# Both ends of a TensorE-bound block: the last 256 tokens in two groups of 128, the first transposes spread between products

## The chip, the cores and the metric

The kernel runs on one core of one Trainium2 chip. The metric is device microseconds (us) of one execution, as the median of several runs. The profile is one execution; its span, from the first to the last instruction, is 1.7 to 2.0 us shorter than the time of the same run. Engines: TensorE (PE; PEld is its weight load), VectorE (DVE), ScalarE (ACT), GpSimd (POOL) and SyncE (SP), whose queue issues most DMAs. All runs here are of the fast state, at a granted clock of 0.995 to 1.0. A ratio is the mean time of one kernel's fast runs over that of the kernel before in the same rounds, so it is not quite the ratio of the medians that are quoted.

## The reference, cut to what matters

```python
def reference(A_x, A_wqkv, A_wo, B_x, B_w1, B_w3, B_w2):
    x  = A_x                                  # (1, 2048, 1024) bf16
    xn = _layernorm(x)
    s  = _A_ref(xn, A_wqkv, A_wo)             # dilated window attention, then @ wo
    g  = _silu(_B_ref(xn, B_w1, B_w3, B_w2))  # gated MLP, width 3584
    return x + s * g
```

Two things of it are concerned: the front (layernorm of the first 512 tokens, their transposes, the first products with `wqkv`) and the very end, where the product with `wo` is multiplied by `g`, the input `x` is added, and the result is written.

## The kernel before

The products are done with a seven-product scheme on halves of the matrices, so that each output piece is a PSUM sum plus an earlier one. Front, end and the statistics of the third and fourth chunk of 512 tokens (condensed; cuts are marked `# ...`):

```python
def tpose(st, a):                     # both halves of a token tile in one PSUM tile
    if st not in tpb:
        tpb[st] = bank2(f"tp{st}")
    for k in range(KH):
        anchor["t"] = nc.tensor.matmul(tpb[st][:, a, k * P:(k + 1) * P], lhsT=..., rhs=ident[:], ...)
# ...
p12(0, 0, one, (0,))
p12(0, 0, one, (1,))
tpose(2, 0); tpose(2, 1); tpose(3, 0); tpose(3, 1)      # third and fourth token tile
untp(2, 0, sc_copy); untp(2, 1, dve_copy)               # copies out of PSUM
untp(3, 0, sc_copy); untp(3, 1, dve_copy)
p12(1, 0, one)
# ...
def tr(c):                            # statistics and transposes of a later chunk
    for sts in ([0, 1], [2, 3]):
        ln_dve(c, sts)
    ln_tr(c, ...)
# ...
for gp in G2:                         # wo: two groups of 256 tokens in each half b
    product(both(pa), gp, a11, b11, True)
    product(both(pe), gp, s1, t1, True)
    flush()                           # last product of the previous group
    # ... act_copy pa -> pb, act_copy pe -> sp5
    product(pbs, gp, s2, t2, False)
    # ... act_copy pb -> su2
    product(both(pe), gp, s4, b22, False);  finished(b, 0, 1, gp, pe, su2[:])
    product(pbs, gp, s3, t3, False);        finished(b, 1, 1, gp, pb, sp5[:])
    product(both(pa), gp, a12, b21, False); finished(b, 0, 0, gp, pa)
    # deferred: product(pbs, gp, a22, t4, False); finished(b, 1, 0, gp, pb)
```

`finished` turns the PSUM sum into bf16 (`d`), multiplies it by `g`, adds `x` (`xw`) and issues the output write. For the last group all of that lies on DVE, with ScalarE for the copies, and the writes go out on the SP queue.

## Time and profile before

| before | us |
|---|---|
| time, median of three runs | 723.84 (723.78 to 724.5) |
| last matmul ends / DVE ends | 715.89 / 718.69 |
| last output write issued / landed | 718.85 / 720.62 |
| span ends | 721.8 |

Read the table from below: after its last matmul the kernel needs another 5.9 us. 3.0 of them pass until the last write is issued, 1.8 until it has landed, and 1.2 until the program ends. The lines that carry the bound and the front are shown with the prediction. One more view of the kernel before matters later: the DMA view of the stretch from 718 to 722 us. Its rows have 40 slices of 0.1 us: the busy share of the DMA engines in tenths, and the rate in GB/s. Below stand the output writes issued in the stretch, with their count, size and time from issue to landing.

```profile
DMA  0000006999999999627995000000000000000000
GB/s 0 0 0 0 0 0 246 399 369 389 389 369 389 389 369 399 205 82 276 379 420 164 10 0 0 0 0 0 0 0 0 0 0 0 0 0 0 0 0 0
...
out_dram<-h_sb SPq DMA_DIRECT2D x2, 128.0 KB, 1.8
```

The data of the last writes come as a block that ends as sharply as it began, at 720.3 us.

### The profile page before, as it was taken

To read this page: it belongs to the slowest core of one execution; us is meant where nothing else is said; L and a number is where in the kernel's file an instruction comes from. 1 tells how busy PE (TensorE), PEld (TensorE's weight loads), DVE (VectorE), ACT (ScalarE), POOL (GpSimd) and SP (SyncE) were. 2 spreads that over 40 slices of the span, in tenths; PEclk is the share of its full clock that TensorE was granted. 3 is DMA by queue.
4 is the path that set the end of the run, shared out by engine and by line. 5 is a ranking of instruction groups with operands and counts; after the bars stand their busy time and mean duration, and the time that the engine had idled before them with its cause. 6 is when DMAs were issued, how large, how long until landed. Compare 5 with 4: busy or idle time off the path is not lost.

```text
span 721.8 us, 8746 instructions
## 1 busy us (share of the span) xinstructions
PE 710.0 (98%) x3313; PEld 346.2 (48%) x3367; DVE 624.9 (87%) x690; ACT 312.9 (43%) x326; POOL 95.7 (13%) x162
## 2 busy tenths in 40 slices
PE   8999999999999999999999999999999999999996
PEld 6655565654444444444444444444444444444442
DVE  7996879779879878978999999969859989999974
ACT  5745334356545456555555312034364573020233
POOL 0011100012300000233111000000435004000011
PEclk9999999999999999999999999999999999999999
DMA  9946257777754523558756547469799444563615
GB/s 337 275 125 182 82 185 228 258 249 238 246 172 153 191 71 117 173 191 268 246 174 216 190 132 250 144 205 385 168 276 336 139 138 150 168 202 129 199 36 108
DMA packets 119193, 139.51 MB, mean 193 GB/s; under 512 B 17648, under 2 KB 94448, under 8 KB 118512
## 3 DMA queue, kind: packets, MB, share of 16 engines
q1 hardware_dynamic: 104608, 97.01, 42.6%
q0 software_dynamic: 14544, 41.95, 18.0%
q8 instruction: 26, 0.43, 0.2%
q14 instruction: 15, 0.12, 0.1%
HBM read 96.21 MB, written 38.80 MB: 187 GB/s over the span
## 4 chain that ended last, share of the span: by engine, by line
PE 95%; ACT 2%; DVE 2%; issue 1%; DMA 0%; DVEq 0%; ACTq 0%
PE bm L151 20%; PE am L151 13%; PE em L151 13%; PE db L151 10%; PE bq L151 9%; PE de L151 7%; PE da L151 7%; PE eq L151 5%; PE aq L151 3%; PE wb L151 2%; PE af L151 2%; PE we L151 2%; PE wa L151 2%; DVE h_sb L236 1%; PE af L1049 1%
## 5 line engine op out<-in xcount | busy, mean ns | idle before, releaser
L151 PEld LDWEIGHTS <-wring 128*128 128x128 f16 (+1 forms) x1792 | 183.4, 102 | 204.3 <-issue 2.2
L151 PEld LDWEIGHTS <-h_sb 128*128 128x128 f16 (+1 forms) x1056 | 109.5, 104 | 118.4 <-issue 0.6
L151 PE MATMUL bm<-xs,wring 128*128 128x512 f16 x504 | 117.4, 379 | 0.2
L151 PE MATMUL am<-xT,wring 128*128 128x512 bf16 x322 | 79.0, 379 | 0.8
L151 PE MATMUL db<-wring,h_sb 128*128 128x512 f16 x336 | 73.2, 379 | 0.0
L481 DVE TENSOR_TENSOR BC<-Ep,vT 128x2048 bf16<-128x2048 bf16 x56 | 66.6, 1217 | 0.1
L426 DVE TENSOR_TENSOR pt<-qt,kT 128x4096 bf16<-128x4096 bf16 x24 | 54.9, 2290 | 0.6
L664 DVE TENSOR_TENSOR um<-em,um 128x1024 f32<-128x1024 f32 x28 | 34.2, 1222 | 21.0 <-PE em L151 13.3
L666 ACT ACTIVATE g<-um 128x1024 bf16<-128x1024 f32 x28 | 29.6, 1057 | 48.6 <-DVE um L664 48.6
L151 PE MATMUL da<-wring,h_sb 128*128 128x512 bf16 x219 | 48.7, 379 | 0.3
L467 POOL DMA_DIRECT2D Ep<-pb x64 | 38.0, 601 | 53.4 <-DVE pb L463 48.1
L151 PE MATMUL bm<-h_sb,wring 128*128 128x512 f16 x168 | 39.7, 379 | 0.0
L151 PE MATMUL em<-xs,wring 128*128 128x512 f16 x168 | 39.7, 379 | 0.0
L151 PE MATMUL em<-xT,wring 128*128 128x512 bf16 x161 | 39.2, 379 | 0.3
L491 DVE TENSOR_TENSOR oT<-oT,BC 128x2048 bf16<-128x2048 bf16 x32 | 39.0, 1219 | 0.3
L161 ACT COPY bm<-am 128x1024 f32<-128x1024 f32 x28 | 27.9, 998 | 25.9 <-PE am L151 25.9
L161 ACT COPY pm<-em 128x1024 f32<-128x1024 f32 x28 | 28.4, 1013 | 20.1 <-PE em L151 20.1
L161 ACT COPY um<-bm 128x1024 f32<-128x1024 f32 x28 | 28.4, 1014 | 18.9 <-PE bm L151 18.9
L685 ACT CAST g<-bm 128x1024 bf16<-128x1024 f32 x28 | 28.3, 1011 | 17.4 <-PE bm L151 17.4
L679 DVE TENSOR_TENSOR h_sb<-bm,pm 128x1024 bf16<-128x1024 f32 x21 | 25.6, 1218 | 5.1 <-PE bm L151 5.0
L489 DVE TENSOR_TENSOR BC<-BC 128x2048 bf16<-128x2048 bf16 x24 | 29.3, 1221 | 0.4
L428 DVE TENSOR_TENSOR pt<-pt 128x2048 bf16<-128x2048 bf16 x24 | 29.3, 1221 | 0.4
(197 smaller groups left out, 993.5 us busy)
## 6 DMA issues: line engine op xcount, KB each, us to landing
wring<-in_B_w_dram SPq DMA_DIRECT2D x61, 512.0 KB, 4.2
wring<-t_dram SPq DMA_DIRECT2D x16, 512.0 KB, 3.8
t_dram<-wring POOLq DMA_DIRECT2D x14, 512.0 KB, 3.8
wring<-t_dram SPq DMA_DIRECT2D x16, 384.0 KB, 4.9
wring<-in_B_w_dram SPq DMA_DIRECT2D x12, 384.0 KB, 4.5
wring<-in_A_x_dram SPq DMA_DIRECT2D x16, 256.0 KB, 4.2
Ep<-pb POOLq DMA_DIRECT2D x64, 64.0 KB, 4.9
wring<-in_A_wo_dram SPq DMA_DIRECT2D x8, 512.0 KB, 5.6
```

What stands on the lines that cost most here:

```text
L151: anchor["pe"] = nc.tensor.matmul(ps, lhsT=lhs[k], rhs=rhs[k], start=(first and k == 0), stop=(k == n - 1), skip_group_check=not first,)
L161: nc.scalar.copy(out=out_, in_=in_)
L426: nc.vector.tensor_mul(p_t[:], q[:], kT[:, :, o:o + CH])
L428: nc.vector.tensor_add(p_t[:, 0:4, :], p_t[:, 0:4, :], p_t[:, 4:8, :])
L467: nc.gpsimd.dma_start(out=pr[c][r:P:NR, :, sq * P:(sq + 1) * P], in_=pb[sq * 32:(sq + 1) * 32, :, :])
L481: nc.vector.tensor_mul(dst, E[:, w, :].unsqueeze(1).to_broadcast([P, n, CH]), vT[:, js, o:o + CH])
L489: nc.vector.tensor_add(B, B, C)
L491: nc.vector.tensor_add(A, A, B if w0 else C)
L664: v = nc.vector.tensor_add(su2[:], pe[:], su2[:])
L666: nc.scalar.activation(out=hl["g"][:, :, CH:], in_=su2[:], func=ACTF.Silu)
L679: anchor["v"] = nc.vector.tensor_add(h[:, :, CH:], pb[:], sp5[:])
L685: nc.scalar.copy(out=hl["g"][:, :, 0:CH], in_=pb[:])
```

## The change

Its intent: the last 256 tokens become two groups of 128, so that DVE has less work left behind the last matmul; the first transposes get PSUM tiles of their own for each half, and the fourth tile's transposes move between products; an early sum of the `q` weights comes sooner; and the statistics of later chunks are ordered behind the sums. In the small groups the third product comes before the second, and the last output piece goes through a ScalarE copy in both halves, where the kernel before multiplied one half straight out of PSUM. The core of the diff, condensed and with cuts:

```diff
-        for gp in G2:
+        for gp, ii in ((0, I), (1, I)) if b == 0 else ((0, I), (1, (0,)), (1, (1,))):
...
+            for k in ("e12", "e22", "e11") if n == 2 else ("e11", "e22", "e12"):
+                steps[k]()
...
-    tpb[0], tpb[1], tpb[2] = [bank2(f"tp{k}") for k in range(3)]
+    lone = [bank2(f"tp{k}") for k in range(3)]
+    tpb[0, 0], tpb[1, 0], tpb[0, 1], tpb[1, 1] = lone[0][:, 0], lone[1][:, 0], lone[2][:, 0], lone[2][:, 1]
...
+    s_q = qkv_sums(wq0, wq1, sq, parts=True)
+    s_q[0]()
...
     tpose(2, 0)
     tpose(2, 1)
+    untp(2, 0, sc_copy)
+    untp(2, 1, dve_copy)
+    p12(1, 0, one[:2])
     tpose(3, 0)
     tpose(3, 1)
...
-    p12(1, 0, one)
+    p12(1, 0, one[2:])
...
     def tr(c):
         for sts in ([0, 1], [2, 3]):
-            ln_dve(c, sts)
+            with behind("ln"):
+                ln_dve(c, sts)
```

More of the change, by code (lines that the diff above doesn't have):

```diff
@@ L890, in wo, with product @@
                         nc.sync.dma_start(out=xw[u, dh], in_=out_rows(x_flat, 1, u, dh, 1))
-        def product(ps, gp, lhs, rhs, first):
-            for i in I:
+        def product(ps, gp, ii, lhs, rhs, first):
+            for n, i in enumerate(ii):
                 g = gp * 2 + i
-                mm(ps[i], [lhs[:, j, g * P:(g + 1) * P] for j in range(4)], [rhs[:, j, :] for j in range(4)], first)
-        both = lambda t: [t[:, i] for i in I]
-        for gp in G2:
-            run_hooks()
-            last = b == 1 and gp == 1
-            pa = bank2(f"wa{b}_{gp}")
-            product(both(pa), gp, a11, b11, True)
-            pe = bank2(f"we{b}_{gp}")
-            product(both(pe), gp, s1, t1, True)
-            flush()
-            pb = [bank2(f"wb{b}_{gp}{i}")[:, i] for i in I] if last else bank2(f"wb{b}_{gp}")
-            for i in I:
-                if last:
-                    act_copy(pb[i], pa[:, i])
-            if not last:
-                act_copy(pb[:], pa[:])
-            pbs = pb if last else both(pb)
-            sp5, su2 = k4(f"wsp{b}_{gp}"), k4(f"wsu{b}_{gp}")
-            act_copy(sp5[:], pe[:])
-            bg((7, 0)[gp] * (1 - b))
-            product(pbs, gp, s2, t2, False)
-            for i in I:
-                if last:
-                    act_copy(su2[:, i], pb[i])
-            if not last:
-                act_copy(su2[:], pb[:])
-            product(both(pe), gp, s4, b22, False)
-            finished(b, 0, 1, gp, pe, su2[:])
-            product(pbs, gp, s3, t3, False)
-            finished(b, 1, 1, gp, pb, sp5[:])
-            product(both(pa), gp, a12, b21, False)
-            finished(b, 0, 0, gp, pa)
-            def tail(gp=gp, pb=pb, pbs=pbs):
-                product(pbs, gp, a22, t4, False)
-                finished(b, 1, 0, gp, pb)
@@ new lines, in product, with half, tail @@
+                mm(ps[:, n], [lhs[:, j, g * P:(g + 1) * P] for j in range(4)], [rhs[:, j, :] for j in range(4)], first)
+        for gp, ii in ((0, I), (1, I)) if b == 0 else ((0, I), (1, (0,)), (1, (1,))):
+            n = len(ii)
+            name = f"{b}_{gp}{ii[0]}"
+            def half(t):
+                return t[:, 0:n]
+            run_hooks()
+            pa = half(bank2(f"wa{name}"))
+            product(pa, gp, ii, a11, b11, True)
+            pe = half(bank2(f"we{name}"))
+            product(pe, gp, ii, s1, t1, True)
+            flush()
+            pb = half(bank2(f"wb{name}"))
+            act_copy(pb, pa)
+            sp5, su2 = half(k4(f"wsp{name}")), half(k4(f"wsu{name}"))
+            act_copy(sp5, pe)
+            bg((7, 0)[gp] * (1 - b))
+            product(pb, gp, ii, s2, t2, False)
+            act_copy(su2, pb)
+            steps = {
+                "e12": lambda: (product(pe, gp, ii, s4, b22, False), finished(b, 0, 1, gp, ii, pe, su2)),
+                "e22": lambda: (product(pb, gp, ii, s3, t3, False), finished(b, 1, 1, gp, ii, pb, sp5)),
+                "e11": lambda: (product(pa, gp, ii, a12, b21, False), finished(b, 0, 0, gp, ii, pa)),
+            }
+            for k in ("e12", "e22", "e11") if n == 2 else ("e11", "e22", "e12"):
+                steps[k]()
+            def tail(gp=gp, ii=ii, pb=pb):
+                product(pb, gp, ii, a22, t4, False)
+                finished(b, 1, 0, gp, ii, pb)
@@ L939, in out_rows @@
         return ap[g0:g0 + 2 * P, dh * CH:(dh + 1) * CH].rearrange("(i p) n -> p i n", p=P)
-    def to_bf16(d, ps, add):
-        if add is None:
-            nc.scalar.copy(out=d, in_=ps[:])
-        elif isinstance(ps, list):
-            for i in I:
-                nc.vector.tensor_add(d[:, i], ps[i], add[:, i])
-        else:
-            nc.vector.tensor_add(d, ps[:], add)
     xw = {}
@@ L958, in residual, with finished @@
                 nc.sync.dma_start(out=out_flat[r0:r0 + n, dh * CH:(dh + 1) * CH], in_=x_flat[r0:r0 + n, dh * CH:(dh + 1) * CH])
-    def finished(b, u, dh, gp, ps, add=None):
-        g = g_tile(b, u, dh, gp)
+    def finished(b, u, dh, gp, ii, ps, add=None):
+        cut = slice(ii[0], ii[-1] + 1)
+        g = g_tile(b, u, dh, gp)[:, cut]
         n = {(0, 0): 0, (1, 1): 2, (0, 1): 4, (1, 0): 0}[u, dh] + gp
-        d = h_sb[:, 16 + 2 * n:18 + 2 * n, CH:]
-        rows_ = out_rows(out_flat, b, u, dh, gp)
+        d = h_sb[:, 16 + 2 * n:18 + 2 * n, CH:][:, cut]
+        rows_ = out_rows(out_flat, b, u, dh, gp)[:, cut]
         with hp():
+            if add is None:
+                nc.scalar.copy(out=d, in_=ps)
+            else:
+                nc.vector.tensor_add(d, ps, add)
+            anchor["v"] = nc.vector.tensor_mul(g, d, g)
             if b == 0 or gp == 0:
-                to_bf16(d, ps, add)
-                anchor["v"] = nc.vector.tensor_mul(g, d, g)
                 nc.gpsimd.dma_start(out=rows_, in_=g, accum_op=ALU.add)
-            elif (u, dh) != (1, 0):
-                to_bf16(d, ps, add)
-                nc.vector.tensor_mul(g, d, g)
-                nc.vector.tensor_add(g, g, xw[u, dh])
+            else:
+                nc.vector.tensor_add(g, g, xw[u, dh][:, cut])
                 nc.sync.dma_start(out=rows_, in_=g)
-            else:
-                for i in I:
-                    if i == 0:
-                        nc.scalar.copy(out=d[:, i], in_=ps[i])
-                    nc.vector.tensor_mul(g[:, i], ps[i] if i else d[:, i], g[:, i])
-                    nc.vector.tensor_add(g[:, i], g[:, i], xw[u, dh][:, i])
-                    nc.sync.dma_start(out=rows_[:, i], in_=g[:, i])
     x_load(0)
@@ L1000, in tpose @@
     def tpose(st, a):
-        if st not in tpb:
-            tpb[st] = bank2(f"tp{st}")
         for k in range(KH):
             anchor["t"] = nc.tensor.matmul(
-                tpb[st][:, a, k * P:(k + 1) * P], lhsT=xt[0][:, st, (a * KH + k) * P:(a * KH + k + 1) * P], rhs=ident[:],
+                tpb[st, a][:, k * P:(k + 1) * P], lhsT=xt[0][:, st, (a * KH + k) * P:(a * KH + k + 1) * P], rhs=ident[:],
                 start=(k == 0), stop=(k == KH - 1), skip_group_check=True,
@@ L1010, in untp @@
         with hp(), behind("a" if eng == sc_copy else "ln"):
-            r = eng(out=xT[:, a, :, st * P:(st + 1) * P], in_=tpb[st][:, a].rearrange("p (k t) -> p k t", k=KH))
+            r = eng(out=xT[:, a, :, st * P:(st + 1) * P], in_=tpb[st, a].rearrange("p (k t) -> p k t", k=KH))
         anchor["ln" if eng == dve_copy else "a"] = r
@@ L1067 @@
     apply(1)
-    tpb[0], tpb[1], tpb[2] = [bank2(f"tp{k}") for k in range(3)]
-    spin(tpb[0], SP0)
+    lone = [bank2(f"tp{k}") for k in range(3)]
+    tpb[0, 0], tpb[1, 0], tpb[0, 1], tpb[1, 1] = lone[0][:, 0], lone[1][:, 0], lone[2][:, 0], lone[2][:, 1]
+    spin(lone[0], SP0)
     tpose(0, 0)
@@ L1072 @@
     with behind("t"):
-        spin(tpb[2], SP1)
+        spin(lone[1], SP1)
     tpose(1, 0)
@@ L1090 @@
     one = [(k,) for k in range(KH)]
-    tpb[3] = bank2("tp3")
     p12(0, 0, one, (0,))
     p12(0, 0, one, (1,))
-    tpose(2, 0)
-    tpose(2, 1)
-    tpose(3, 0)
-    tpose(3, 1)
-    untp(2, 0, sc_copy)
-    untp(2, 1, dve_copy)
-    untp(3, 0, sc_copy)
-    untp(3, 1, dve_copy)
-    p12(1, 0, one)
-    p12(0, 1, one, (0,))
-    p12(0, 1, one, (1,))
-    p12(1, 1, [range(KH)])
     sk = rows(4, 6, FP16).rearrange("p (q k n) -> p q k n", q=3, k=4)
@@ L1109 @@
     sq = [sq[:, q] for q in range(3)]
+    s_q = qkv_sums(wq0, wq1, sq, parts=True)
+    s_q[0]()
+    late = [bank2(f"tp{k}") for k in (3, 4)]
+    for st in (2, 3):
+        tpb[st, 0], tpb[st, 1] = late[st - 2][:, 0], late[st - 2][:, 1]
+    tpose(2, 0)
+    tpose(2, 1)
+    untp(2, 0, sc_copy)
+    untp(2, 1, dve_copy)
+    p12(1, 0, one[:2])
+    tpose(3, 0)
+    tpose(3, 1)
+    untp(3, 0, sc_copy)
+    untp(3, 1, dve_copy)
+    p12(1, 0, one[2:])
+    p12(0, 1, one, (0,))
+    p12(0, 1, one, (1,))
+    p12(1, 1, [range(KH)])
     b12 = rows(12, 2).rearrange("p (k n) -> p k n", k=KH)
@@ L1149 @@
     pf[0, 0], pf[0, 1] = pf[0], pf[1]
-    s_q = qkv_sums(wq0, wq1, sq, parts=True)
-    s_q[0]()
     s_q[1]()
```

## The prediction

> **What bounds the kernel now.** I read the busy table of the page first, then the chain that ended last (whole, and its last 40 us), then the timeline of the first 36 us and of the last 20 us, because the change touches only those two ends.
>
> ```profile
> PE 710.0 (98%) x3313; PEld 346.2 (48%) x3367; DVE 624.9 (87%) x690; ACT 312.9 (43%) x326; POOL 95.7 (13%) x162
> PE 95%; ACT 2%; DVE 2%; issue 1%; DMA 0%; DVEq 0%; ACTq 0%
> ```
>
> TensorE is the bound: 98% busy, 95% of the chain. The change keeps every matmul, so only three things can move: holes between matmuls, the time before TensorE starts for good, and the time after its last matmul. From the starts of single matmul records I take the pitch: 0.216 us for 512 columns (the chain shows "1.73 PE we L151 x8"), 0.109 us for 256, 0.056 us for a 128-column transpose. Starts later than the pitch allows are holes. After 12 us the holes above 0.03 us sum to about 2 us in the whole trace, so with both ends less than 1% can be had.
>
> The front (timeline):
>
> ```profile
> 10.12 0.55 DVE L236 TENSOR_SCALAR wring<-wring,h_sb 128x1024 bf16<-128x1024 bf16 x1
> 10.77 0.55 DVE L236 TENSOR_SCALAR wring<-wring,h_sb 128x1024 bf16<-128x1024 bf16 x1
> ...
> 11.83 5.41 PE L1049 MATMUL af<-xT,wring 128*128 128x256 bf16 x48
> ...
> 32.17 0.69 DVE L248 BATCH_NORM_STATS2 stats<-wring 128x6 f32<-128x512 bf16 x1 [1.24 <-DMA wring<-in_A_x_dram]
> 32.78 0.41 DVE L236 TENSOR_TENSOR xs<-xT,xs 128x512 f16<-128x512 bf16 x1
> ...
> 33.33 1.89 PE L151 MATMUL bq<-xs,h_sb 128*128 128x512 f16 x8
> ```
>
> The two DVE lines normalise the third and fourth token tiles; they end at 10.67 and 11.32, and their transposes start at 10.72 and 11.37, each 0.05 us later. The fourth tile's transposes could have started at 11.18: a hole of 0.19 us. Later DVE sits 1.24 us waiting for a DMA in a statistics instruction that stands AHEAD of a short subtraction (32.78), and the product at 33.33 needs that subtraction: by pitch it would have started at 33.07, a hole of 0.26 us.
>
> The tail (end of the chain, in order of time):
>
> ```profile
> 709.33 0.96 PE wb L151 x4
> 710.29 0.02 issue
> 710.32 0.59 ACT wsu L161
> 710.91 0.02 issue
> 710.93 1.23 DVE h_sb L948
> ...
> 717.60 0.42 DVE h_sb L979
> 718.02 0.34 DVE h_sb L980
> 718.35 0.33 DVEq L1278
> ```
>
> From 710.9 the chain is no longer TensorE but DVE. TensorE's last matmul ends at 715.89, DVE runs without a real break to 718.69, the last output DMA is issued at 718.85, lands at 720.62, and the span ends at 721.8.
>
> **What the Trainium skill says.** "Perfetto Trace Analysis", section "Per-instruction lifecycle" (Tensor Engine part): "ACT/DVE/GPSIMD are strict FIFO". The trace agrees: the subtraction at 32.78 could not pass the statistics held up by a DMA. "VectorE: DVE Perf Modes", section "The perf-mode tier table": `tensor_tensor` runs at twice the rate on bf16 in SBUF (1224 ns at 2048) and at the single rate with any PSUM operand. The trace has 1217 ns for 2048 bf16, and 1.23 us for 1024 from PSUM. Same page, section on the TRN2 errata: each instruction pays a fixed extra, so halves cost more than half. The trace: 0.69 us for 1024 bf16, 0.42 for 512; from PSUM 1.23 and 0.68; ScalarE copies 1.01 and 0.59. "DMA: Bandwidth & Descriptors", section "Anatomy of one DMA": about 2 us fixed, stated for the GpSimd path. The trace for the SP queue: 2.2 us for the 256 KB output writes, 1.8 for 128 KB, so size hardly shortens the last landing.
>
> **The change part by part.** The built order of the changed kernel shows what really moves.
>
> 1. First transposes, tiles of their own per half. The first copy out of PSUM (7.42) then waits for 4 transposes, not 8; the second waits for the half of the next tile. By the trace's 0.057 us per transpose and 0.59 per copy, the first product starts near 8.5 in place of 8.72. But next on TensorE, as before, come the third tile's transposes, bound to DVE's end at 10.67. The 0.2 us just widens that wait. **Worth 0.**
>
> 2. Fourth tile's transposes between products. New order: transposes of tile three (10.72 to 11.18 by pitch), 8 matmuls (0.87 us, to 12.05), transposes of tile four. Those now come long after DVE's 11.32. The hole goes: **-0.19 us**. Three conditions, all tight but met: weights for those 8 matmuls landed at 9.53 and 10.18; the second ScalarE snapshot copy, which must precede the third of them, ends at 11.34, and that matmul is due at 11.40; the copy out of the fourth tile's transposes ends near 13.3 by my sum (last transpose 12.67, copy 0.59), and the product that reads it is due at 13.38.
>
> 3. An early weight sum on DVE (1.22 us) moves ahead of two PSUM copies on DVE, filling their 0.68 us wait. DVE is not the bound there; its copies are wanted only at about 15.1 and end near 13.9. **Worth 0.**
>
> 4. The statistics of the third chunk are put behind the sums. In the built order the subtraction follows its partner directly, so it ends near 31.25 in place of 33.18, and the product starts by pitch: **-0.26 us**. DVE also loses the 1.24 us DMA wait (all those loads land by 37.5, and it gets there about 36). At 50.68 the trace has a hole of 0.08 us behind a late DVE addition; DVE being a microsecond ahead, it should go: **-0.08 us**. One weight load changes places with a DMA transpose on the SP queue; DVE has 5.74 us of slack before 71.65, so I count 0. The rest of the middle stands in unchanged order.
>
> 5. The tail, in two groups of 128 tokens. Same 56 matmuls after 703.55, in eights and fours (0.863 us per four). Walking the built order with the durations above: first small group's products start at 701.83 and 702.69, then come the previous group's last eight at 703.55, then 705.28, 706.14, 707.03, 707.90; second small group 708.76, 709.62, the first's last four 710.48, then 711.35, 712.21, 713.07, 713.94. The very last four need DVE to have read their PSUM half: that addition starts at about 714.25 (behind a multiplication that itself waits for a ScalarE copy ending 713.87) and ends 714.93, so they start at 714.97 against 714.80 by pitch, and end at 716.0. TensorE thus ends 0.1 us LATER than before. What shrinks is DVE behind it. Starting 714.25: PSUM addition (0.60 to the next start), residual addition (0.34), PSUM addition (0.60), two multiplications (0.68), residual addition (0.34), then the last multiplication, whose ScalarE copy (716.04 to 716.62) is ready, at 716.80, and two additions: end 717.90. Last issue 718.04 against 718.85: **-0.81 us**. Cost: DVE gets 4 more instructions, ScalarE 3, the SP queue 3 more issues (0.37 us each), all beside matmuls.
>
> Sum: 0.19 + 0.26 + 0.08 + 0.81 = 1.34 us; 723.84 - 1.34 = **722.5 us**.
>
> **Rivals.** (a) DVE's backlog in the tail stays: before, six DVE instructions start at or after 715.8; if the small pieces, with their fixed costs, pile up, the 0.8 us is eaten. Against it: each small group has 6.9 us of matmuls (32 by 0.216) and 3.9 us of DVE (two PSUM additions at 0.60 from start to start, eight bf16 operations at 0.34). If true: 723.3. (b) TensorE takes over with new waits: groups of four leave 0.86 us between a product and the ScalarE copy (0.59) that its successor but one needs; I see about 0.03 us at 707.03 and 0.17 at the end, but two or three more stalls of 0.2 would give 723.1. (c) The front becomes slower: a late snapshot or copy stalls TensorE by up to 0.2 us, and part 2 is worth nothing: 722.7. (d) The full intent of the front comes true, all holes of 6.8 to 11.4 (0.84 + 0.26 + 0.19) gone: 722.5 less the 0.84 and 0.26 not counted above, 721.4. Against it: DVE's end at 10.67 does not move, its work from 3.31 on being almost gapless.
>
> **Range and chances.** The runs before spread from 723.78 to 724.5. Terms of mine could each be off by 0.2 to 0.4 us, and the middle may gain or lose a hole of 0.3. I take 721.7 to 723.5. Two per cent is 14.5 us, ten times anything here: faster 0.005, within 0.99, slower 0.005.
>
> **What would show it.** Tile three's transposes still start near 10.7, tile four's near 12.05, the first 512-column product starts near 16.9 in place of 17.08; no DMA wait of DVE near 32; the product of 33.33 starts near 32.9 without a hole; the last matmul ends about 0.5 us earlier in absolute time than before (715.89 + 0.1 - 0.53 = 715.5); from there to the last issue 2.0 us, against 3.0. The prediction is wrong if the front's holes reappear elsewhere, if the span from the last matmul to the end stays 5.9 us, or if the middle, which I hold fixed, moves by more than 0.3 us.

## The result, and the profile after

The changed kernel took 723.24 us (median of four runs, 723.06 to 723.99), the kernel before 723.84 beside it; the ratio is 0.9992, with a 95% interval of 0.9974 to 1.0009. So 0.60 us were gained where 1.34 had been predicted. The time lies in the range, but most of the predicted gain is missing. The interval includes 1, so by the times alone even the 0.60 us are not clear of noise; what follows rests on the profiles.

Now the same places of the profile as before. The front and the statistics, in the timeline (start, duration, engine, line, operation):

```profile
10.79 0.62 PE L985 MATMUL tp<-ident,wring 128*128 128x128 bf16 x8 [0.19 <-DVE wring L236]
...
12.12 0.61 PE L985 MATMUL tp<-ident,wring 128*128 128x128 bf16 x8
```

```profile
31.06 0.43 DVE L236 TENSOR_TENSOR xs<-xT,xs 128x512 f16<-128x512 bf16 x1
...
35.95 1.87 DVE L248 BATCH_NORM_STATS2 stats<-wring 128x6 f32<-128x512 bf16 x3
```

```profile
32.94 1.89 PE L151 MATMUL bq<-xs,h_sb 128*128 128x512 f16 x8
```

The third tile's transposes still wait for DVE, the fourth's no longer do. The subtraction on DVE stands at 31.06 in place of 32.78, ahead of the statistics and without a wait for a DMA, and the product that needs it starts at 32.94 in place of 33.33. Next the end of the chain, in order of time:

```profile
711.90 0.88 PE wa L151 x4
712.78 0.02 issue
712.80 0.59 ACT h_sb L956
...
716.38 0.34 DVE h_sb L959
716.72 0.33 DVE h_sb L963
717.05 0.34 DVEq L1264
```

The last write is issued at 717.50, 1.35 us earlier than before (718.85), and the last matmul ends at 715.52. Up to here the change gained what was predicted. But the span is 721.5 us, only 0.3 us shorter. The last landing is at 720.50, 3.00 us after the issue in place of 1.77. The DMA view from 718 to 721 us (slices of 0.075 us) shows what happens there; below it is the line of the instruction queue:

```profile
DMA  9997238998410020001101100000000000000000
GB/s 382 410 369 260 55 109 300 382 355 314 151 28 0 0 109 0 0 0 27 14 0 14 14 0 14 14 14 0 0 0 0 0 0 0 0 0 0 0 0 0
...
q14 instruction: 1, 0.01, 0.6%
```

The second block, up to 718.9 us, is the last write. It does not end sharply. At 719.05 there is one slice of 109 GB/s: times 0.075 us that is 8,192 bytes, the one packet of the instruction queue (q14). Then, from 719.35 to 720.03, single packets trickle: 27 + 14 x 6 GB/s, or eight packets of 1 KB. The write has 128 such packets, eight for each of sixteen DMA engines. So, as I read it, one engine was held by the fetch and did its share of the write after it, 1.1 us after the others. The packet records carry no engine number, so that it is one engine is inferred; but the fetch packet ends at 719.36, the first late packet starts there, and each of the eight starts within 0.02 us of the end of the one before it, as on one engine (the same in e1_again, e3_tail and e9_before_pad6 below, where the fetch packet took 0.40, 0.55 and 0.77 us). What that engine did between 718.4 and 719.05 us is not seen. In the page of the whole kernel this queue has one fetch more than before:

```profile
q14 instruction: 15, 0.12, 0.1%
```

```profile
q14 instruction: 16, 0.13, 0.1%
```

The first line is of the kernel before, the second of the changed one. Before, the fetch came at 723.5 us, when the span was over. DVE has 830 instructions in the built program before and 836 in the changed one (the traces have records of 828 and 834: seven more that compute, one semaphore instruction less). Six of the queue's earlier packets fall near DVE's 62nd, 185th, 319th, 448th, 557th and 692nd instruction, in steps of 109 to 135, so the next was to be expected near the 832nd: the old program ended just short of it, the new one crosses it with its last few. This was picked out of fifteen packets; the others do not follow DVE's count (some fall at ScalarE's 64th, 190th, 319th and 446th instruction), so it is a guess until DVE's count alone is changed.

The Trainium skill bears on this: "Runtime: NRT & Kernel Launch", section "Instruction fetch mechanics", says that the sequencer fetches its next block of instructions by a DMA queue of its own while it executes, and calls the cost "mostly hidden". The trace agrees on the queue. DVE itself was not held up by this fetch (its last instruction ended at 717.39, before it); whether the fetch cost something elsewhere is to be tested below.

### The profile page after: what moved, and what is told of

Its sections match the earlier page's. It is cut to its first block, busy times and chain, and to the rows that moved or that the text cites. A ratio compares the mean times of both kernels' runs of the same rounds, so it can differ in the third digit from the quotient of the medians.

```text
span 721.5 us, 8817 instructions
## 1 busy us (share of the span) xinstructions
PE 713.2 (99%) x3367; PEld 346.3 (48%) x3367; DVE 625.5 (87%) x697; ACT 314.0 (44%) x329; POOL 95.7 (13%) x162
## 4 chain that ended last, share of the span: by engine, by line
PE 95%; ACT 2%; DVE 2%; DMA 0%; issue 0%; DVEq 0%; ACTq 0%
PE bm L151 20%; PE am L151 13%; PE em L151 13%; PE db L151 10%; PE bq L151 9%; PE de L151 7%; PE da L151 7%; PE eq L151 6%; PE aq L151 3%; PE wb L151 2%; PE af L151 2%; PE wa L151 2%; PE we L151 2%; DVE h_sb L236 1%; PE af L1030 1%; DMA wring<-in_A_x_dram 0%
```

## The experiments

Twelve kernels ran, in three calls of four, each call on another chip and with five rounds beside the kernel before (723.74, 723.90 and 724.08 us, medians of nine in the three calls; so medians of different calls are comparable to some 0.3 us, and a gain is always taken against the same call). Only six of the intervals below leave out 1: those of e4, e6, e9, e10, e11 and e12. The other differences are not clear of noise as times and are read from the profiles. The kernel before was not profiled again.

| run | edit | median us | against before | ratio (95%) |
|---|---|---|---|---|
| e1_again | the change | 723.40 | -0.34 | 0.9993 (0.9981 to 1.0006) |
| e2_front | front and statistics only | 723.48 | -0.26 | 0.9995 (0.9981 to 1.0009) |
| e3_tail | two last groups only | 723.83 | +0.09 | 1.0001 (0.9988 to 1.0013) |
| e4_pad20 | the change, 20 memsets | 722.78 | -0.96 | 0.9986 (0.9973 to 0.9998) |
| e5_before_pad8 | before, 8 memsets | 724.15 | +0.25 | 1.0002 (0.9988 to 1.0015) |
| e6_tail_pad20 | last groups, 20 memsets | 722.66 | -1.24 | 0.9981 (0.9968 to 0.9993) |
| e7_ln | statistics only | 723.40 | -0.50 | 0.9993 (0.9980 to 1.0005) |
| e8_pool | e4 with GpSimd in the tail | 724.52 | +0.62 | 1.0006 (0.9994 to 1.0019) |
| e9_before_pad6 | before, 6 memsets | 725.16 | +1.08 | 1.0015 (1.0002 to 1.0027) |
| e10_tp | transposes only | 728.54 | +4.46 | 1.0060 (1.0047 to 1.0073) |
| e11_ln_tail_pad20 | last groups, statistics, 20 memsets | 722.90 | -1.18 | 0.9984 (0.9971 to 0.9998) |
| e12_pad20_again | e4 again | 722.82 | -1.26 | 0.9984 (0.9971 to 0.9997) |

### Where did the tail's gain go?

Theory A: a fetch of DVE's instructions falls into the last write. Rivals: the late landing was chance, or four short writes queue behind each other.

**The change once more.** No edit.

> The changed kernel once more, unchanged. Theory A (an instruction fetch of 8 KB lands among the packets of the last output write because the DVE program is six instructions longer): the last output write takes 3.0 us from issue to landing again, with one 8 KB packet on the instruction queue near 719 us; time 723.2. Rival B (that landing of 3.0 us was chance): this profile shows 1.7 to 1.8 us and no 8 KB packet after 716 us, and the span is near 720.4.

Measured: the 8,192-byte packet again at 719.1 us, the last landing 2.90 us after its issue, time 723.40. It was not chance.

**The front without the tail.** The last groups as before, all else changed.

> Only the two front parts of the change (transposes in their new tiles and order, statistics put behind the sums), the tail as before. Expected from the profile: TensorE runs 0.47 us ahead at 700 us (holes of 0.19, 0.26 and 0.08 gone, the start 0.06 later), the tail as before with its last landing 1.8 us after issue: span 721.3, time 723.4. Rival (the front is absorbed later, the whole gain is the tail's): 723.8.

Measured: no packet before 723.3 us, landing 1.76 us after the issue, time 723.48. The holes at 11.4, 33.3 and 50.7 us were gone. But the last matmul came only 0.24 us earlier than before (715.65), not 0.47: the first transposes started 0.29 us later in this profile.

**The tail without the front.** The two last groups alone.

> Only the tail part. Six DVE instructions more than before, as in the changed kernel. Theory A: last issue 0.9 us earlier than before (717.97 for 718.85), but the last landing takes about 3.0 us, so span 721.7 to 722.0 and time 723.6 to 723.9: nothing gained. Rival B (late landing was chance): span 720.9, time 723.0.

Measured: packet at 719.9, landing 2.95 us after the issue, time 723.83: alone, the tail gains nothing. Its last matmul ended at 716.62 and its last write was issued at 718.60, 1.98 us later against 2.96 before: the gain was there and was taken back. (The issue itself was expected at 717.97; this profile's first transposes started 0.68 us later than before's.)

**The fetch moved away.** The whole change, with one-column memsets on DVE at the very front, where DVE has time:

```diff
     nc.vector.memset(warm[:], 0.0)
+    pad = const.tile([P, 20], FP32, name="pad")
+    for i in range(20):
+        nc.vector.memset(pad[:, i:i + 1], 0.0)
```

> The changed kernel with 20 memsets of one column on DVE at its start, in the 2 us in which DVE waits for the first tokens; nothing else differs in any engine's order. It shifts the place in the DVE program at which 8 KB more of it are fetched. Theory A: the 8 KB packet comes some 20 DVE instructions earlier (before 715 us), the last output write lands 1.7 to 1.8 us after its issue, span 720.3, time 722.2. Rival C (the last landing is long because four output writes stand close behind each other): unchanged, 3.0 us, 723.2.

Measured: with 856 DVE instructions the packet came at 709.9 us, the last landing 1.76 us after its issue, time 722.78, 0.96 us under the kernel before. The DMA view of its end (717 to 721.5 us, slices of 0.11 us):

```profile
DMA  9300000000007995017994599710000000000000
GB/s 328 100 0 0 0 0 0 0 0 0 0 9 273 364 346 164 9 46 264 364 337 146 200 364 346 237 28 0 0 0 0 0 0 0 0 0 0 0 0 0
```

The last block ends sharply again. The four short writes are all there, so they are not the cause; twenty useless instructions made the kernel 0.62 us faster than the same change without them. The landing alone gained 1.14, and 722.2 had been expected; the rest is a last matmul 0.90 us later than in e1_again, 0.51 of it at a hole at 506 us that is looked at below. That DVE instructions alone moved the packet shows also whose fetch it is: by the trace's records it comes after DVE's 831st in this kernel as in the three above.

**The kernel before with eight memsets.** Now the other direction: can the old kernel be given the fault? The same edit with 8 in place of 20.

> The kernel before with eight one-column DVE memsets added at the front, 838 DVE instructions in place of 830, nothing else. Theory A (an 8 KB instruction fetch for DVE falls into the last output write when DVE's 832nd place comes up in the tail): an 8 KB packet on the instruction queue between about 717 and 720 us, the last landing about 2.9 us after its issue in place of 1.8, the time 0.6 to 1.2 us longer, 724.3 to 724.9. Rival B (the late landing comes from the four separate last writes of the changed kernel, which this kernel has not): landing 1.8 us after the issue, time 723.7 to 724.0 as before.

Measured: the packet came at 719.2 us as expected, but the landing was only 1.94 us and the time 724.15. The size was missed. As I read it, the reason is the order of things: here the packet came 0.5 us before the last write was issued, at 719.69, so it had passed when that write's data were due. The write issued before it, at 718.55, did land 2.55 us after its issue, where writes of that size (256 KB) take 2.2 to 2.3.

**The kernel before with six memsets.** 836 DVE instructions, as many as the changed kernel.

> The kernel before with six one-column DVE memsets at the front: 836 DVE instructions, as many as the changed kernel has. With eight (838) the fetch fell 0.5 us before the last write was issued, and that write landed 1.94 us after its issue. Two instructions fewer should bring the fetch later, 0.3 to 1.6 us after the last issue, as in the changed kernel. Theory A (the fetch harms a write whose data are due when it passes): last landing 2.4 to 3.0 us after its issue, time 724.3 to 724.9, above the kernel with eight. Rival (the fetch harms only the changed kernel's short last writes): landing at most 2.0 us, time 723.8 to 724.2.

Measured: the packet at 720.8, 1.0 us after the last issue (719.82), the landing 2.78 us after it, time 725.16: 1.08 us more than the kernel before, where eight memsets cost 0.25. The DMA view of its end (718 to 723.9 us, slices of 0.15 us):

```profile
DMA  9997000000299999998993000100000000000000
GB/s 340 354 340 257 14 0 0 0 0 0 76 354 340 340 333 347 333 354 271 375 333 98 0 0 21 14 7 14 0 0 0 0 0 0 0 0 0 0 0 0
...
q14 instruction: 1, 0.01, 0.8%
```

There is the trickle again: 21 + 14 + 7 + 14 GB/s in slices of 0.1475 us are eight packets of 1 KB. Six idle memsets cost the old kernel more than the changed kernel gained. How much of the 1.08 us is the fetch's is not settled by the time: the landing is 1.01 us later than before's, but in this profile, the slowest of the five executions, the last matmul also came 0.96 us later, by loads that landed late at 7, 21.6 and 32.6 us. All runs in one table (from the issue and packet records):

| run | DVE instructions | packet after the last issue, us | landing after the last issue, us |
|---|---|---|---|
| before | 830 | 4.7 (after the span) | 1.77 |
| e2_front, e7_ln, e10_tp | 830 | 4.7 to 4.9 (after the span) | 1.76 to 1.78 |
| after | 836 | 1.55 | 3.00 |
| e1_again | 836 | 1.4 | 2.90 |
| e3_tail | 836 | 1.3 | 2.95 |
| e9_before_pad6 | 836 | 1.0 | 2.78 |
| e5_before_pad8 | 838 | -0.5 | 1.94 |
| e4_pad20, e6_tail_pad20, e11_ln_tail_pad20, e12_pad20_again | 856 | about -8.7 | 1.75 to 1.76 |

(e8_pool, below, has the packet 10.5 us before its last issue and lands in 1.76.)

**The tail alone, fetch moved away.** e3_tail with the 20 memsets.

> The tail part of the change alone, with 20 one-column DVE memsets at the front so that the fetch falls well before the last write. Theory A (the tail saves what was worked out for it, 0.8 us, and the fetch took it back): last matmul to last issue 2.0 us, landing 1.8 us after the issue, time 0.7 to 0.9 us under the kernel before, 722.8 to 723.1. Rival (the tail alone gains nothing, because its start or its small pieces cost what it saves): within 0.2 us of the kernel before, as the tail alone without the memsets was.

Measured: 722.66, 1.24 us under the kernel before; last matmul to last issue 1.98 us, landing 1.75. More than the 0.7 to 0.9 expected. One part was not foreseen: from the last landing to the end of the span every kernel with the old tail takes 1.14 to 1.16 us, every one with the new tail 0.96 to 0.98. So the tail saves 0.98 us up to the last issue and 0.18 behind the landing. In this profile the span, 720.9, is only 0.9 under before's 721.8, because the last matmul came 0.34 us later than before's. Against e3_tail, the same edit without the memsets, 1.20 of the 1.33 us between the two gains stand in the landing.

### What is the front worth?

**The statistics alone.** Only the `with behind("ln")` around `ln_dve`.

> Only the last hunk: the statistics of the third and fourth chunks put behind the weight sums; no other part, 830 DVE instructions, no fetch near the end. By the prediction's terms the holes of 0.26 us at 33.3 and of 0.08 us at 50.7 go and the 0.26 and 0.19 us holes at 10.7 and 11.4 stay: time 0.34 us under the kernel before, about 723.4. Rival: the waits at the statistics were hidden and TensorE meets another wait of the same size before 72 us: within 0.1 us of the kernel before, and a new hole between 33 and 72 us.

Measured: 723.40, 0.50 us under before (0.34 expected). The holes at 33.3 and 50.7 are gone, no new one shows up to 72 us. The interval of the ratio includes 1 (0.9980 to 1.0005), and in the profile the last matmul comes 0.23 us earlier than before's: the mechanism is shown, the size is not.

**The transposes alone.** All hunks of the front except that one.

> Only the front's transposes: the first ones into PSUM tiles of their own, the fourth tile's between products, the early weight sum; not the statistics behind the sums, not the tail. 830 DVE instructions, no fetch near the end. By the prediction's terms the 0.19 us hole at 11.4 goes and nothing else: 723.5 to 723.8, that is 0.0 to 0.3 us under the kernel before. Rival (the early products meet weights that have not landed, as seen at 9.0 to 9.9 in two runs of the changed kernel): new holes at 9 to 10 us that sum to more than 0.2 us, time 723.8 to 724.2.

Measured: 728.54 us (726.95 to 729.23), 4.46 us slower than before. Neither theory had that (the rival's holes at 9.4 to 9.6 us are there, 0.34 us in sum, and are the smaller part). The timeline of this run:

```profile
27.83 0.96 DVE L236 TENSOR_TENSOR xs<-h_sb,xT 128x1536 f16<-128x1536 bf16 x1 [0.25 <-DMA h_sb<-wring]
31.76 0.69 DVE L248 BATCH_NORM_STATS2 stats<-wring 128x6 f32<-128x512 bf16 x1 [2.97 <-DMA wring<-in_A_x_dram]
32.37 0.94 DVE L236 TENSOR_TENSOR xs<-xT,xs 128x1536 f16<-128x1536 bf16 x1
```

```profile
34.84 1.92 PE L151 MATMUL eq<-xs,h_sb 128*128 128x512 f16 x8 [3.27 <-DVE xs L236]
```

The scheduler put the first statistics of the third chunk three instructions further ahead than in the kernel before: before the 1536-column subtraction, where the load it needs lands only at 31.74. DVE, which works in order, stands still for 2.97 us, and TensorE for 3.27 (3.44 counted by the pitch of its matmuls; before, the hole there was 0.26). These 3.2 us more are the whole difference of this profile's span (725.0) to before's; it is the fastest of the five executions, and what the others lost beyond it is not seen. e2_front is this kernel with the edit of the statistics, and took 723.48. So that edit is not one more small gain: it is what makes the other front edits safe. That the early weight sum, and not the transposes, lets the statistics come forward is plausible, but no run separates the two.

**Everything but the transposes.** The last groups, the statistics and the 20 memsets.

> The tail, the statistics behind the sums and the 20 memsets, without the front's transposes. If the terms add up (tail 0.8 to 1.2, statistics 0.3 to 0.5): 722.2 to 722.6, under the whole change with memsets (722.8) by what the front's transposes cost. Rival (the parts don't add, run to run differences in loads hide the small ones): 722.6 to 723.0, no different from the whole change with memsets in this call.

**The whole change with memsets, beside it.**

> The whole change with 20 memsets once more, on the same chip as the kernel without the front's transposes. Theory: 722.5 to 723.0 as before (722.78), last landing 1.8 us after its issue. Its profile had a hole of 0.73 us at 506 behind a weight load that landed late; if that is chance, it is there or not there independent of the edit; if it belongs to the memsets, it is there again with 0.4 us or more.

Measured: 722.90 and 722.82. On the same chip, in the same rounds, the transposes are worth 0.08 us or nothing. The matmul records say why. Two lines of e12_pad20_again, of the early products and of ScalarE's copies of their sums out of PSUM (the prediction's "snapshots"):

```profile
9.71 1.31 PE L1033 MATMUL af<-xT,wring 128*128 128x256 bf16 x10 [0.22 <-DMA wring<-in_A_wqkv_dram]
```

```profile
10.47 1.18 ACT L235 COPY oT<-af 128x512 f32<-128x512 f32 x2
```

The whole change has no hole at the fourth tile any more. But the products on the second token tile reached a weight before its load had landed: a hole of 0.38 us at 9.71. It makes the second snapshot late (it ends at 11.65), and the third of the eight matmuls that now stand between the transposes, which must not start before that copy, starts at 11.70: a new hole of 0.11 us. e1_again, e4_pad20 and e8_pool show the same chain, with holes of 0.58 to 0.67 us between 9.0 and 10.3 and then 0.16 to 0.17 us, each time 0.05 to 0.06 us after the copy's end. In the changed kernel's first profile the early holes were 0.13 us in sum, the copy ended at 11.41, and no such hole followed. The early holes come and go with the landing of the first loads; the first transposes move by up to 0.7 us between runs as well (6.76 to 7.44). And where they start late, as in e11_ln_tail_pad20 (7.22), the third tile's transposes no longer wait for DVE, the fourth's follow without a hole, and there is nothing to save:

```profile
10.91 1.10 PE L990 MATMUL tp<-ident,wring 128*128 128x128 bf16 x16
```

The profile of e12_pad20_again has also holes of 0.40 us at 21.4 (a weight load of `h_sb` that landed late) and 0.18 at 32.0; e11_ln_tail_pad20 has 0.11 at 31.5 alone. The hole at 21 us stands in most profiles of the second and third call, with the new transposes (e8, e10, e12) and without (e5, e6, e9), so I do not put it down to them.

The hole of 0.73 us at 506 us in e4_pad20 was not there in e12_pad20_again (0.22, as in the kernel before): it stood behind DVE work that waited 1.09 us for a weight load. So it does not come with the memsets every time. But e8_pool has it too (0.75) and e5_before_pad8 in part (0.41), and no kernel without memsets has more than 0.29; whether memsets have a share in it stays open.

The parts do not add: the tail with memsets saved 1.24, the statistics 0.50, together they saved 1.18. With 0.3 us between the medians of calls and the holes just named, this stays open.

### A version that goes further?

The whole change with the 20 memsets beats both kernels (by 0.96 and 1.26 us against before; the changed kernel saved 0.60 and 0.34). In its end DVE is the chain from 714.5 to 718.2 us, so I tried to relieve it: in the last group one multiplication and three additions go to GpSimd, and the last product is multiplied straight out of PSUM.

```diff
+            end = ii == (1,) and (u, dh)
+            if end == (1, 0):
+                d = ps
-            if add is None:
+            elif add is None:
                 nc.scalar.copy(out=d, in_=ps)
...
-            anchor["v"] = nc.vector.tensor_mul(g, d, g)
+            anchor["v"] = (nc.gpsimd if end == (1, 1) else nc.vector).tensor_mul(g, d, g)
...
-                nc.vector.tensor_add(g, g, xw[u, dh][:, cut])
+                (nc.gpsimd if end and end != (1, 0) else nc.vector).tensor_add(g, g, xw[u, dh][:, cut])
```

> The changed kernel with the 20 memsets, and in its very last group of 128 tokens one multiplication and three residual additions moved from DVE to GpSimd, the last product multiplied by DVE straight out of PSUM in place of a ScalarE copy and a multiplication. Theory (DVE's queue behind the last matmuls sets the last issue): with GpSimd pieces of about 0.6 us DVE ends about 717.6 against 718.15, last matmul to last issue 1.4 us in place of 2.0, time about 722.3, 0.5 us under the changed kernel with memsets alone (722.8). Rival (GpSimd pieces take over 1 us, or slow DVE's bf16 work beside them): the last GpSimd addition ends after DVE, last issue later than 2.0 us after the last matmul, time 722.8 or more.

Measured: 724.52 us, 0.62 slower than before. The rival was right, twice over: the last write was issued 3.76 us after the last matmul. From its timeline:

```profile
716.41 1.14 POOL L965 TENSOR_TENSOR h_sb<-h_sb 128x512 bf16<-128x512 bf16 x1
...
716.59 1.25 DVE L965 TENSOR_TENSOR h_sb<-h_sb 128x512 bf16<-128x512 bf16 x1
717.63 2.50 POOL L969 TENSOR_TENSOR h_sb<-h_sb,xw 128x512 bf16<-128x512 bf16 x2
...
718.47 0.65 DVE L969 TENSOR_TENSOR h_sb<-h_sb,xw 128x512 bf16<-128x512 bf16 x1
```

A piece of 128x512 that DVE does in 0.42 us takes GpSimd 1.14 to 1.32. And while GpSimd reads, DVE's own bf16 multiplication takes 1.25 us in place of 0.42: it lasts until shortly after GpSimd's instruction is done. The Trainium skill has this: "SBUF — State Buffer", section "Who interferes with whom", says that a DVE instruction with two SBUF inputs contends with a GpSimd instruction that reads SBUF, and that it is a lock, not a shared rate. The trace agrees; DVE's addition at 715.86, one of whose inputs is in PSUM, took its usual 0.69 us beside a GpSimd addition that ended at 716.45.

## Why the prediction was right or wrong

The time was in its range (723.24 in 721.7 to 723.5), but the gain was 0.60 us and not 1.34. That the time fell into a range 1.8 us wide is in part luck: no reason given for the range covers what took the gain. By its own steps:

- **Step 1, first transposes, worth 0.** Held: the third tile's transposes start at 10.79 (foretold: near 10.7).
- **Step 2, fourth tile between products, 0.19 us.** The mechanism held: start 12.12 (near 12.05), no hole, the first 512-column product at 16.95 (near 16.9). Its worth in time did not show: 0.08 us between e11_ln_tail_pad20 and e12_pad20_again. Of the three conditions called "tight but met", taken from one trace, the second fails where a load lands late: the second snapshot copy, counted to end at 11.34, ended at 11.61 to 11.99 in e1, e4, e8 and e12, and the third matmul waited 0.11 to 0.17 us for it. And where the first transposes start late, there is no hole to fill (e11).
- **Step 3, early weight sum, worth 0.** True in the whole change. Steps 1 to 3 without step 4 let the scheduler move the statistics ahead and cost 4.46 us (e10_tp); which of the three does it is not separated.
- **Step 4, statistics behind the sums, 0.26 and 0.08 us.** The mechanism held: both holes gone. Measured alone it gave 0.50 us, which is not clear of noise. What I missed is that it also guards steps 1 to 3.
- **Step 5, the tail, 0.81 us.** Held to the last issue and failed behind it. Last matmul at 715.52 (foretold 715.5), from there to the last issue 1.98 us (2.0). The term that failed is the last landing, taken over from the kernel before as 1.8 us ("size hardly shortens the last landing"): it was 3.00 us, for an instruction fetch that DVE's six new instructions brought into the last write. I had counted four new DVE instructions in the tail (the pages have seven more that compute, 697 for 690) as a cost "beside matmuls", and not what the sheer number of them does. My own test for a wrong prediction, "if the span from the last matmul to the end stays 5.9 us", came true: 721.48 - 715.52 = 5.96.

The sum in the profile: 1.35 us gained up to the last issue, 1.23 lost in the landing, 0.18 gained after it (1.16 to 0.98 us from the landing to the end of the span); that is 0.30 us of span. With the fetch out of the way the change is worth 0.96 and 1.26 us, near the predicted 1.34; near by a different sum, for the fourth tile's 0.19 us mostly did not come and the 0.18 behind the landing were not foreseen. Of the rivals, (a) and (d) did not come, (b) only with its 0.03 and 0.145 us at 706.6 and 714.5, which were in the sum; (c) came true in four of the seven profiles with the new transposes (e1, e4, e8, e12): a snapshot copy made late by late weights, 0.11 to 0.17 us. None of the four named what took the gain.

## What to carry to other kernels

When a tail is shortened and the span does not follow, look at what moves in the DMA view behind the last issue, and count the instructions of each engine: a fetch near the end can be shifted by a few idle instructions, in either direction, and a difference of 1 us between two versions may be nothing else. Judge the parts of a change with a scheduler in between both alone and together, for one part may only be harmless because of another. And where a part only removes a wait of 0.2 us, ask what the engine will meet next.

## What the Trainium skill lacked or had wrong

- "Runtime: NRT & Kernel Launch", section "Instruction fetch mechanics", gives blocks of 16 KiB (256 instructions) and calls the fetch "mostly hidden". In this trace one instruction queue moves packets of 16,384 bytes (26 in both kernels), but the queue on which DVE's fetches come moves packets of 8,192, which is 128 instructions by the page's own ratio; the steps found on DVE are 109 to 135. DVE was not held up, but a fetch 1.0 to 1.55 us after the issue of the last output write delayed that write's landing from 1.77 to between 2.78 and 3.00 us, a cost that the page does not have.
- "DMA: Bandwidth & Descriptors", section "Anatomy of one DMA": gives about 2.0 us fixed plus the size, for the GpSimd path. The undisturbed last writes, 128 KB from the SP queue, landed in 1.75 to 1.78 us all told. The page does not name an instruction fetch as something that can stand in front of a part of a transfer; eight late packets of 1 KB held up the whole write by 1.0 to 1.2 us.
